# Expert stage of an attention, mixture-of-experts and feed-forward kernel: another place for the decoding operations, for GpSimd's weight blocks and for the decoded part's subtraction

## Chip, core and metric

The kernel runs on one core of one Trainium2 chip. The metric is the device time of one execution in microseconds (us), as the median of several runs. Five engines work side by side, each through its own instructions in order: TensorE (PE; its weight loads are listed as PEld), VectorE (DVE), ScalarE (ACT), GpSimd (POOL) and SyncE (SP), which here only issues DMAs.

## What is computed

Three layers follow each other. A gated linear attention over 4 x 8 heads of 768 positions gives 3072 tokens of 384 values. A mixture of experts sends each token that is not skipped to one of 8 experts. A feed-forward layer with a maximum over three products ends the kernel. The change is in the second layer, where some weights of the third are decoded on the side.

```python
for e in range(E):                      # 8 experts, w1[e] 384 x 1024, w2[e] 1024 x 384
    mask = e_idx == e
    h = np.maximum(xc[mask] @ w1[e], 0.0)
    y[mask] = gate_w[mask, None] * (h @ w2[e])
out[do_compute] = xc + y
...
h = np.maximum(np.maximum(x @ w1, x @ w2), x @ w3)   # 384 x 768 each
return h @ w_out                                     # 768 x 384
```

## The kernel before

Every float32 product is made of three products of float32r values: a tensor is split into a high part, which ScalarE writes as a cast copy, and a low part, source minus high part, written by VectorE or GpSimd. `split` (L119) does both; its two operations carry the lines L120 and L121.

**Expert stage.** The loop at L765 makes 66 steps; step s serves expert e = s // 8 and block f = s % 8 of 128 hidden units, and has up to 256 token slots as columns. In a step TensorE runs `gemm1(s)`, nine matmuls (L661 to L663) into one of three PSUM banks named `ph`, and `gemm2(s - 2)`, six matmuls into two banks `po` (L679 to L681). After `gemm1`, ScalarE writes `hh`, the high part of the rectified result (L666), and VectorE writes `hl`, the low part (L667). In steps f = 4, 5 and 6 `xprep` (L638) also transposes one third of the next expert's tokens and splits it into `xh` and `xl`; the one of f = 5 takes a `ph` bank. So the bank of `gemm1` of block 4 comes back at `gemm1` of block 6, once `hl` of block 4 is written. At f = 1 the expert before is finished: two VectorE operations write its rows `o` from PSUM (L688), and GpSimd scatters them with two indirect DMAs (L689). After the last expert `merge` (L728) forms its tokens' rows directly for the third layer.

**Weights.** In step s `wsplit` (L440) splits the weight block of step s + 3 into `wh` and `wl`, 128 x 768 each. A set of f says whether VectorE or GpSimd subtracts; ScalarE always casts. Four blocks share one buffer `raw` of 1.5 MB, of which there are two; at f = 0 and f = 4, behind the split of a buffer's last block, `wload` (L431) loads it anew for the blocks five steps ahead.

**Decoding.** `mdecs` (L601) is a generator that decodes the third layer's weights in 12 units of 128 x 768, in pieces that end at a `yield`. A unit takes: an absolute value on ScalarE (L101, in `begin`, which also issues the load `rm` of the next unit), two one-input operations on VectorE (`decode_exp`, L105 and L106, called exponent operations below), two operations with two inputs (`decode_bits`, L111 and L112, called bit operations), a cast copy to `mh` on ScalarE (L621), and the subtraction that gives `ml` (L624), on GpSimd for the first seven units (`EARLY`). Stores of `mh` and `ml` (L628) follow for some units. `decode_to(n)` (L760) runs the generator up to piece n; the loop calls it at the head of a step, with a count that grows by one every two steps from step 3 on, so that a unit takes eight steps.

The order on each engine is the order in which the Python code issues instructions.

Of the kernel before, what the change touches and what calls it, by code (L numbers as in the profile page):

```python
# [9 lines left out]
F32 = mybir.dt.float32  # L10
F32R = mybir.dt.float32r
BF16 = mybir.dt.bfloat16
I32 = mybir.dt.int32
U32 = mybir.dt.uint32
AF = mybir.ActivationFunctionType
ALU = mybir.AluOpType
# [25 lines left out]
NTILE = N // 128  # L42
EW = 768
AHEAD = 3
DEC = 3
UN = 768
ORDER = [(w, u) for u in range(2) for w in range(3)] + [(3, 0), (3, 1), (0, 2), (1, 2), (2, 2), (3, 2)]
EARLY = 7
# [31 lines left out]
K_LO = 2.0 ** -15  # L80
K_HI = 122880.0
# [3 lines left out]
def tile_gla_moe_moe2(ctx, tc, akq, vp, rp, wgt, cst, io, ew, md, out):  # L85
    nc = tc.nc
    V, A, G, T, SY = nc.vector, nc.scalar, nc.gpsimd, nc.tensor, nc.sync
# [8 lines left out]
    def words(raw):  # L96
        wd = raw.rearrange("p (n t) -> p n t", t=2)
        return wd[:, :, 0], wd[:, :, 1]

    def decode_abs(t, raw):  # L100
        A.activation(t, words(raw)[1], AF.Abs)  # L101

    def decode_exp(t):
        ti = t.bitcast(I32)
        V.tensor_scalar(t, t, K_LO, K_HI, ALU.max, ALU.min)  # L105
        V.tensor_scalar(ti, ti, 0x07FFFFFF, 3, ALU.bitwise_and, ALU.logical_shift_left)  # L106

    def decode_bits(t, raw):
        lo, hi = words(raw)
        ti = t.bitcast(I32)  # L110
        V.scalar_tensor_tensor(ti, hi.bitcast(I32), -0x40000000, ti, ALU.bitwise_and, ALU.bitwise_or)  # L111
        V.scalar_tensor_tensor(ti, lo.bitcast(I32), 29, ti, ALU.logical_shift_right, ALU.bitwise_or)  # L112

    def decode(t, raw):
        decode_abs(t, raw)
# [3 lines left out]
    def split(h, l, src, eng=None):  # L119
        A.copy(h, src)  # L120
        (eng or V).tensor_tensor(l, src, h.bitcast(F32), ALU.subtract)  # L121

    with tc.manual_schedule():
# [307 lines left out]
        def wload(n):  # L431
            rw[n] = rawp.tile([128, 4 * EW], F32, name="raw")
            SY.dma_start(out=rw[n], in_=ew[n // 2, :, n % 2 * 4 * EW:(n % 2 + 1) * 4 * EW])
# [6 lines left out]
        def wsplit(s, eng=None):  # L440
            h, l = (wsl.tile([128, EW], F32R, name=f"w{a}") for a in "hl")
            split(h, l, rw[s // 4][:, s % 4 * EW:(s % 4 + 1) * EW], eng)
            wr[s] = h, l
# [144 lines left out]
        rm = {}  # L588
# [7 lines left out]
        def mload(i):  # L596
            rm[i] = rmp.tile([128, 2 * UN], F32, name="rm")
            w, u = ORDER[i]
            SY.dma_start(out=rm[i].bitcast(I32), in_=md[3 * w + u].bitcast(I32))

        def mdecs():  # L601

            ts = {}

            def begin(i):
                if i < len(ORDER):
                    if i + 1 < len(ORDER):
                        mload(i + 1)
                    ts[i] = rmp.tile([128, UN], F32, name="dt")
                    decode_abs(ts[i], rm[i])  # L610

            begin(0)
            yield
            for i, (w, u) in enumerate(ORDER):
                z = slice(u * UN, (u + 1) * UN)
                t, h, l = ts[i], mh[w][:, z], ml[w][:, z]
                decode_exp(t)
                yield
                decode_bits(t, rm[i])
                yield  # L620
                A.copy(h, t)  # L621
                begin(i + 1)
                yield
                (G if i < EARLY else V).tensor_tensor(l, t, h.bitcast(F32), ALU.subtract)  # L624
                for k in range(k3 if w < 3 else 0):
                    if (w, k) in ONE:
                        for j, m in enumerate((mh, ml)):
                            SY.dma_start(out=wv[ONE[w, k]][:, 2 * u:2 * u + 2, j],  # L628
                                         in_=mv(m[w], k)[:, 2 * u:2 * u + 2].bitcast(F32))
                    if u == 2:  # L630
                        A.copy(fv(blk[w, k])[:, 4:], t.rearrange("p (f k c) -> k p f c", f=2, k=k3)[k])
                yield

        def xload(e):
            xs_[e] = xp.tile([128, 2, XW], F32, name="xs", bufs=3)
            SY.dma_start(out=xs_[e], in_=slots[e * CAP:(e + 1) * CAP, :].rearrange("(m p) d -> p m d", p=128))

        def xprep(e, k):  # L638
            xs = xs_[e]
            if k < 0:  # L640
                ix_[e] = xp.tile([128, 2, 1], I32, name="ix", bufs=4)
                V.tensor_copy(ix_[e], xs[:, :, DM + 1:DM + 2])
                return
            if k == 0:
                xh_[e] = xhp.tile([128, k3, CAP], F32R, name="xh")
                xl_[e] = xhp.tile([128, k3, CAP], F32R, name="xl")
            pt = (bank(ps_h, "ph") if k == 1 else bank(ps_t, "pt"))[:, 0:CAP]
            for m in range(2):
                T.transpose(pt[:, m * 128:(m + 1) * 128], xs[:, m, k * 128:(k + 1) * 128], ident)
            split(xh_[e][:, k, :], xl_[e][:, k, :], pt)  # L650
# [61 lines left out]
        def gstart(k):  # L712
            pm.append(bank(ps_o, f"po{k}") if k < 2 else bank(ps_t, "pt"))
            for c in range(4):
                T.matmul(pm[k][:, c * 128:(c + 1) * 128], xg_[0][:, c, k * 128:(k + 1) * 128], ident,
                         start=(c == 0), stop=False)
# [43 lines left out]
        def decode_to(n):  # L760
            while ndec[0] < n:
                ndec[0] += 1
                next(dec, None)

        for s in range(ns + LAG):  # L765
            e, f = divmod(s, nf1)
            if s >= DEC:
                decode_to(min(s - DEC + 1, 58) * (4 * EARLY + 1) // 58 + max(s - 60, 0))
            if s < ns:
                if 4 <= s + AHEAD < ns:  # L770
                    wsplit(s + AHEAD, V if f in (0, 2, 4, 5, 7) or s < 2 else G)
                if s and (s + AHEAD) % 4 == 3 and (s + AHEAD) // 4 + 2 < 2 * NE:
                    wload((s + AHEAD) // 4 + 2)
                if f == XL and e + 2 < NE:
                    xload(e + 2)
                if s == 0:
                    xload(1)
                    xload(0)
                gemm1(s)
            if s in (ns - 1, ns):  # L780
                gstart(s - ns + 1)
            if s == ns + 1:
                gstart(2)
            if s >= LAG:
                gemm2(s - LAG)
            x0 = XP if e else 5
            if e + 1 < NE and x0 <= f < x0 + k3:
                xprep(e + 1, f - x0)
            if f == IX and e < NE:
                xprep(e, -1)  # L790
            if s == ns - 7:
                gload(0)
            if s == ns - 3:
                sel = select()
            if s == 9:
# [114 lines left out]
        lo, hi = {}, {}  # L910
# [55 lines left out]
        def alljobs():  # L966
            yield from wjobs()
            yield GAP
            xslots()
            yield from xjobs(0)  # L970
# [3 lines left out]
        def pump(us):  # L974
            debt[0] += us
            while debt[0] > 0:
                c = next(jobs, None)
                debt[0] = 0.0 if c is None else debt[0] - c
# [110 lines left out]
        for g in range(ng):  # L1089
            for f in range(nf2):  # L1090
                if g == 1 and f == 0:
                    rawt += [rawp.tile([128, 8 * DM], F32R, name="raw") for _ in range(2)]
                gemm1(g, f)
                if g == 0:
                    decode_to(4 * EARLY + 10 + 4 * f)
                    if f == 3:
                        decode_to(99)
                        rmt += [rmp.tile([128, 2 * UN], F32, name="rm") for _ in range(2)]
                        for _ in jobs:
                            pass  # L1100
                        jobs, debt[0] = alljobs(), 0.0
                if g == 0 and f == 0:
                    xgload(0, 1)
                    xgload(1, 3)
                if g == 0 and f == nf2 - 1:
                    xgload(0, 2, A)
                if pend is not None:
                    gemm2(*pend)
                    pump(PUMP[3] if g or f > 3 else 0)
                pend = (g, f)  # L1110
                if g == 0 and 2 <= f < 2 + k3:
                    pt = bank(ps_t, "pt")
                    tr(0, f - 2, pt)
                    split(xh_[1][:, f - 2, :], xl_[1][:, f - 2, :], pt)
                if g == 1 and f == LOADAT:
                    wdload(0)
# [250 lines left out]
```

## Time and profile before

| quantity | value |
|---|---|
| median of 3 runs | 587.48 us (587.32 to 589.78) |
| profiled execution, own time | 588.17 us |
| its span, first to last instruction | 586.3 us |
| TensorE busy | 563.4 us (96%) |
| VectorE busy | 440.5 us (75%) |
| ScalarE busy | 296.7 us (51%) |
| GpSimd busy | 247.6 us (42%) |
| mean granted TensorE clock | 0.996 of full speed |

The profile is one execution. Every row has a start and a duration in us from the span's start, and idle time is put down to the instruction that ended it. TensorE's ends are modelled, so its busy time can hide a short stop; the distance between the first matmuls of two steps does not. The expert stage runs from about 142 to 297 us.

### The profile page before, as it was taken

How to read it: one execution, taken by the hardware profiler on the slowest of the kernel's cores; microseconds unless marked ns; L12 is line 12 of the kernel's file. 1: busy time of each engine (PE TensorE's matmuls, PEld its weight loads, DVE VectorE, ACT ScalarE, POOL GpSimd, SP SyncE). 2: the span in 40 equal slices, each digit the busy share in tenths (PEclk: the TensorE clock that was granted, in tenths of full speed). 3: DMA queues.
4: the chain of work that ended last, by engine and by line, in shares of the span. 5: the costliest groups of instructions: out<-in, count | busy, mean ns of one | idle time of the engine just before them, and what ended most of it. 6: DMA issues, size and time to landing. Idle time of an engine off the chain costs nothing.

```text
span 586.3 us, 10712 instructions
## 1 busy us (share of the span) xinstructions
PE 563.4 (96%) x3995; PEld 504.0 (86%) x3995; DVE 440.5 (75%) x747; ACT 296.7 (51%) x602; POOL 247.6 (42%) x202
## 2 busy tenths in 40 slices
PE   6999999999999989998999999999999999999995
PEld 3888888888899989998978788888878899888895
DVE  7899999977788898889768898593767684766700
ACT  2655575654566556665324435454453474454310
POOL 6554598752465346544321213122464401455410
PEclk8999999999999999999999999999999999999999
DMA  8889998935687879784508239515663623565011
GB/s 314 308 237 351 306 309 320 331 116 190 239 256 288 300 259 312 263 308 169 180 20 267 74 108 354 212 39 207 210 242 137 217 108 137 187 213 192 0 56 59
DMA packets 50973, 123.04 MB, mean 210 GB/s; under 512 B 4546, under 2 KB 38832, under 8 KB 47328
## 3 DMA queue, kind: packets, MB, share of 16 engines
q1 hardware_dynamic: 47824, 116.65, 57.8%
q0 software_dynamic: 2560, 4.83, 2.2%
q10 hardware_dynamic: 528, 0.79, 0.5%
q8 instruction: 33, 0.54, 0.4%
q14 instruction: 28, 0.23, 0.1%
HBM read 93.03 MB, written 32.28 MB: 214 GB/s over the span
## 4 chain that ended last, share of the span: by engine, by line
PE 58%; DVE 11%; issue 4%; ACT 3%; DMA 3%; POOL 1%; DVEq 0%; ACTq 0%; POOLq 0%
PE po L1004 3%; PE po L1005 3%; PE po L1006 3%; PE ph L1004 3%; PE ph L1005 3%; PE ph L1006 3%; PE ph L661 3%; PE po L681 2%; PE ph L662 2%; PE po L679 2%; PE po L680 2%; PE ph L663 2%; DVE wl L121 2%; PE ph L843 2%; PE ph L842 2%
## 5 line engine op out<-in xcount | busy, mean ns | idle before, releaser
L121 POOL TENSOR_TENSOR wl<-raw,wh 128x768 fp32r<-128x768 f32 x26 | 49.2, 1893 | 64.0 <-ACT wh L120 63.9
L121 DVE TENSOR_TENSOR wl<-raw,wh 128x768 fp32r<-128x768 f32 x38 | 57.5, 1513 | 11.7 <-ACT wh L120 11.7
L120 ACT CAST wh<-raw 128x768 fp32r<-128x768 f32 x64 | 53.4, 834 | 21.7 <-DMA raw<-in_ew_dram 11.1
L661 PE MATMUL ph<-xh,wh 128*128 128x256 f32 x192 | 56.5, 294 | 3.6 <-DVE hl L667 3.5
L662 PE MATMUL ph<-xl,wh 128*128 128x256 f32 x192 | 54.4, 283 | 0.4 <-DVE xl L121 0.3
L663 PE MATMUL ph<-xh,wl 128*128 128x256 f32 x192 | 54.3, 283 | 0.0
L679 PE MATMUL po<-wh,hh 128*128 128x384 f32 x128 | 43.5, 340 | 0.0
L681 PE MATMUL po<-wh,hl 128*128 128x384 f32 x128 | 43.2, 338 | 0.0
L680 PE MATMUL po<-wl,hh 128*128 128x384 f32 x128 | 43.1, 337 | 0.0
L661 PEld LDWEIGHTS ph<-xh,wh 128*128 128x128 f32 x192 | 36.5, 190 | 5.4 <-DVE hl L667 5.2
L268 PE MATMUL ps<-q,k 64*128 64x128 f32 x384 | 32.9, 292 | 8.1 <-POOL q L243 4.1
L228 POOL TENSOR_TENSOR k<-akq,sf 128x512 f32<-128x512 f32 x24 | 28.5, 1187 | 24.6 <-DVE sf L225 16.1
L268 PEld LDWEIGHTS ps<-q,k 64*128 64x128 f32 x384 | 27.0, 193 | 12.4 <-POOL q L243 5.2
L662 PEld LDWEIGHTS ph<-xl,wh 128*128 128x128 f32 x192 | 36.4, 190 | 0.8 <-DVE xl L121 0.8
L663 PEld LDWEIGHTS ph<-xh,wl 128*128 128x128 f32 x192 | 36.4, 189 | 0.0
L419 POOL DMA_INDIRECT slots<-xr,si x24 | 24.4, 1015 | 27.2 <-DVE xr L416 11.9
L667 DVE SCALAR_TENSOR_TENSOR hl<-ph,hh 128x256 fp32r<-128x256 f32 x64 | 26.5, 417 | 9.2 <-ACT hh L666 8.9
L666 ACT ACTIVATE hh<-ph 128x256 fp32r<-128x256 f32 x64 | 24.5, 383 | 14.9 <-PE ph L663 13.6
L225 DVE TENSOR_TENSOR_SCAN sf<-akq,pcs 128x520 f32<-128x520 f32 x24 | 29.4, 1224 | 3.0 <-DMA akq<-in_akq_dram 2.7
L239 DVE TENSOR_TENSOR_SCAN ap<-akq,pcs 128x521 f32<-128x521 f32 x24 | 29.8, 1241 | 2.2
L274 DVE TENSOR_TENSOR sm<-ps,cs 128x512 f32<-128x512 f32 x48 | 30.3, 672 | 0.0
L243 POOL TENSOR_TENSOR q<-akq,ap 128x512 f32<-128x512 f32 x24 | 28.4, 1183 | 4.5 <-DVE ap L239 2.8
(659 smaller groups left out, 1721.9 us busy)
## 6 DMA issues: line engine op xcount, KB each, us to landing
raw<-in_ew_dram SPq DMA_DIRECT2D x15, 1536.0 KB, 6.6
akq<-in_akq_dram SPq DMA_DIRECT2D x22, 772.5 KB, 6.6
rm<-in_md_dram SPq DMA_DIRECT2D x12, 768.0 KB, 7.8
mh<-wd SPq DMA_DIRECT2D x7, 1024.0 KB, 4.9
ml<-wd SPq DMA_DIRECT2D x7, 896.0 KB, 6.8
raw<-wd SPq DMA_DIRECT2D x6, 1024.0 KB, 5.0
raw<-wd SPq DMA_DIRECT2D x6, 896.0 KB, 6.5
vt<-in_vp_dram SPq DMA_DIRECT2D x24, 200.0 KB, 6.8
```

The lines of the kernel that those rows point to most:

```text
L120: A.copy(h, src)
L121: (eng or V).tensor_tensor(l, src, h.bitcast(F32), ALU.subtract)
L268: T.matmul(ps[i][:, p, :], kh[j][r0:r0 + 64, p, :], qh[j][r0:r0 + 64, p, :], start=True, stop=True)
L661: T.matmul(ph, wh[:, z], xh_[e][:, k, :], start=(k == 0), stop=False)
L662: T.matmul(ph, wh[:, z], xl_[e][:, k, :], start=False, stop=False)
L663: T.matmul(ph, wl[:, z], xh_[e][:, k, :], start=False, stop=(k == k3 - 1))
L679: T.matmul(po, hh[:, zm], wh, start=(f == 0), stop=False)
L680: T.matmul(po, hh[:, zm], wl, start=False, stop=False)
L681: T.matmul(po, hl[:, zm], wh, start=False, stop=(f == nf1 - 1))
L1004: T.matmul(bk, uh, vh, start=start, stop=False, skip_group_check=not start)
L1005: T.matmul(bk, uh, vl, stop=False, **more)
L1006: T.matmul(bk, ul, vh, stop=True, **more)
```

## The change

The generator's pieces for the first seven units are made smaller and are placed by block: one VectorE operation at a time. `decode_to` moves from the head of a step to its end, behind `gemm2` and `xprep`, starts at step 8 and runs one piece a step, so that a unit fills the eight steps of one expert: exponent operations at f = 1 and f = 2, bit operations at f = 3 and f = 5, `begin` at f = 6, and at f = 0 of the next expert the copy, GpSimd's subtraction and the stores. GpSimd's weight blocks are split at f = 1, 4 and 6, where they were at f = 1, 3 and 6.

```diff
-DEC = 3
+DEC = 8
...
-    def decode_exp(t):
+    def decode_exp(t, parts=(0, 1)):
         ti = t.bitcast(I32)
-        V.tensor_scalar(t, t, K_LO, K_HI, ALU.max, ALU.min)
-        V.tensor_scalar(ti, ti, 0x07FFFFFF, 3, ALU.bitwise_and, ALU.logical_shift_left)
+        if 0 in parts:
+            V.tensor_scalar(t, t, K_LO, K_HI, ALU.max, ALU.min)
+        if 1 in parts:
+            V.tensor_scalar(ti, ti, 0x07FFFFFF, 3, ALU.bitwise_and, ALU.logical_shift_left)
...
-                decode_exp(t)
-                yield
-                decode_bits(t, rm[i])
-                yield
-                A.copy(h, t)
-                begin(i + 1)
-                yield
-                (G if i < EARLY else V).tensor_tensor(l, t, h.bitcast(F32), ALU.subtract)
+                if i < EARLY:
+                    decode_exp(t, (0,))
+                    yield
+                    decode_exp(t, (1,))
+                    yield
+                    decode_bits(t, rm[i], (0,))
+                    yield
+                    yield
+                    decode_bits(t, rm[i], (1,))
+                    yield
+                    begin(i + 1)
+                    yield
+                    yield
+                    A.copy(h, t)
+                    G.tensor_tensor(l, t, h.bitcast(F32), ALU.subtract)
+                else:
...
         for s in range(ns + LAG):
             e, f = divmod(s, nf1)
-            if s >= DEC:
-                decode_to(min(s - DEC + 1, 58) * (4 * EARLY + 1) // 58 + max(s - 60, 0))
             if s < ns:
                 if 4 <= s + AHEAD < ns:
-                    wsplit(s + AHEAD, V if f in (0, 2, 4, 5, 7) or s < 2 else G)
+                    wsplit(s + AHEAD, V if f in (0, 2, 3, 5, 7) or s < 2 else G)
...
                 xprep(e, -1)
+            if s >= DEC:
+                decode_to(min(s - DEC + 1, 8 * EARLY + 1) + max(s - 60, 0))
...
-                    decode_to(4 * EARLY + 10 + 4 * f)
+                    decode_to(8 * EARLY + 10 + 4 * f)
```

How the instructions stand on two engines, before and now (line numbers of the changed kernel are higher: its L125 is L121, L635 is L624, L687 is L667, L106 and L108 are L105 and L106, L114 is L111, L708 and L709 are L688 and L689).

GpSimd before, through most of an expert, from the block at f = 1 to that of f = 6:

```order
L121 TENSOR_TENSOR wl_2741<-raw_2592,wh_2740 128x768
L689 DMA x2_63<-o_2764,ix_2683 3072x384
L689 DMA x2_63<-o_2769,ix_2683 3072x384
L121 TENSOR_TENSOR wl_2806<-raw_2592,wh_2805 128x768
L624 TENSOR_TENSOR ml1_2220<-dt_2531,mh1_2216 128x768
L121 TENSOR_TENSOR wl_2901<-raw_2715,wh_2900 128x768
```

GpSimd now, from the end of f = 0 to the block at f = 6:

```order
L635 TENSOR_TENSOR ml0_2219<-dt_2477,mh0_2215 128x768
L125 TENSOR_TENSOR wl_2737<-raw_2581,wh_2736 128x768
L709 DMA x2_63<-o_2760,ix_2671 3072x384
L709 DMA x2_63<-o_2765,ix_2671 3072x384
L125 TENSOR_TENSOR wl_2824<-raw_2581,wh_2823 128x768
L125 TENSOR_TENSOR wl_2887<-raw_2705,wh_2886 128x768
```

The subtraction of the decoded part stood behind the block of f = 3, and stands now ahead of the block of f = 1 and of the two indirect DMAs.

VectorE before, from f = 0 to f = 5 (`o` are the finished expert's rows):

```order
L121 TENSOR_TENSOR wl_3203<-raw_2963,wh_3202 128x768
L667 SCALAR_TENSOR_TENSOR hl_3219<-ph_3208,hh_3218 128x256
L667 SCALAR_TENSOR_TENSOR hl_3243<-ph_3232,hh_3242 128x256
L688 SCALAR_TENSOR_TENSOR o_3252<-po0_3042,xs_2656 128x384
L688 SCALAR_TENSOR_TENSOR o_3257<-po1_3043,xs_2656 128x384
L121 TENSOR_TENSOR wl_3268<-raw_3083,wh_3267 128x768
L667 SCALAR_TENSOR_TENSOR hl_3282<-ph_3271,hh_3281 128x256
L667 SCALAR_TENSOR_TENSOR hl_3308<-ph_3297,hh_3307 128x256
L121 TENSOR_TENSOR wl_3323<-raw_3083,wh_3322 128x768
L667 SCALAR_TENSOR_TENSOR hl_3339<-ph_3328,hh_3338 128x256
L121 TENSOR_TENSOR xl_3349<-pt_3350,xh_3348 128x256
L121 TENSOR_TENSOR wl_3356<-raw_3206,wh_3355 128x768
```

VectorE now, from the finished expert's rows at f = 1 to the block of f = 5:

```order
L708 SCALAR_TENSOR_TENSOR o_3248<-po0_3034,xs_2644 128x384
L708 SCALAR_TENSOR_TENSOR o_3253<-po1_3035,xs_2644 128x384
L106 TENSOR_SCALAR dt_3166<-dt_3166 128x768
L125 TENSOR_TENSOR wl_3260<-raw_3072,wh_3259 128x768
L687 SCALAR_TENSOR_TENSOR hl_3274<-ph_3263,hh_3273 128x256
L108 TENSOR_SCALAR dt_3166<-dt_3166 128x768
L125 TENSOR_TENSOR wl_3287<-raw_3072,wh_3286 128x768
L687 SCALAR_TENSOR_TENSOR hl_3301<-ph_3290,hh_3300 128x256
L114 SCALAR_TENSOR_TENSOR dt_3166<-rm_2919,dt_3166 128x768
L687 SCALAR_TENSOR_TENSOR hl_3328<-ph_3317,hh_3327 128x256
L125 TENSOR_TENSOR xl_3338<-pt_3339,xh_3337 128x256
L125 TENSOR_TENSOR wl_3345<-raw_3196,wh_3344 128x768
```

The weight block ahead of `hl` of block 4 is gone from there; three decoding operations, which stood elsewhere in the expert, now stand between the rows `o` and that `hl`, with one weight block at f = 2 and one at f = 3.

ScalarE before, at the stage's end, up to the merge (`mh` is the copy, `dt` the absolute value, `hh` of steps 61 to 63):

```order
L666 ACTIVATE hh_4061<-ph_4051 128x256
L666 ACTIVATE hh_4083<-ph_4073 128x256
L666 ACTIVATE hh_4112<-ph_4102 128x256
L621 CAST mh3_2218<-dt_3994 128x768
L101 ACTIVATE dt_4127<-rm_3992 128x768
L666 ACTIVATE hh_4139<-ph_4129 128x256
L732 ACTIVATE wh_4095<-po0_4014,xs_3635 128x384
```

ScalarE now, in the same place:

```order
L686 ACTIVATE hh_4074<-ph_4064 128x256
L101 ACTIVATE dt_4087<-rm_3893 128x768
L686 ACTIVATE hh_4106<-ph_4096 128x256
L634 CAST mh3_2218<-dt_3895 128x768
L686 ACTIVATE hh_4130<-ph_4120 128x256
L641 CAST mh3_2218<-dt_4087 128x768
L101 ACTIVATE dt_4163<-rm_4085 128x768
L752 ACTIVATE wh_4091<-po0_4006,xs_3621 128x384
```

The copy and the absolute value of the last two units stood ahead of the last `hh`, and stand now behind it, next to the merge.

## Rows read from the trace of the kernel before

**Rows 1.** Stretches by expert: length, PE, PEld, DVE, ACT, POOL busy, clock, DMA, GB/s:

```profile
159.42:178.07 18.65, 18.34 (x130) 17.70 (x129) 16.72 (x32) 11.94 (x22) 9.59 (x6) 1.00 0.83 280
...
196.14:216.02 19.88, 18.23 (x128) 17.64 (x127) 17.45 (x26) 11.33 (x21) 9.37 (x6) 1.00 0.83 292
216.02:233.70 17.68, 17.68 (x127) 17.58 (x127) 15.17 (x22) 11.79 (x21) 10.04 (x6) 1.00 0.81 280
...
251.91:271.79 19.88, 18.23 (x128) 17.64 (x127) 17.02 (x25) 11.33 (x21) 9.34 (x6) 1.00 0.84 296
```

**Rows 2.** Timeline of TensorE, steps' first matmuls: start, duration, engine; bracketed, idle before:

```profile
210.88 0.39 PE L661 MATMUL ph<-xh,wh 128*128 128x256 f32 x1 [1.35 <-DVE hl L667]
...
224.55 0.29 PE L661 MATMUL ph<-xh,wh 128*128 128x256 f32 x1
...
229.16 0.36 PE L661 MATMUL ph<-xh,wh 128*128 128x256 f32 x1
```

**Rows 3.** Timeline of VectorE, then of GpSimd, expert 3, from block 3 on:

```profile
206.19 4.30 DVE L121 TENSOR_TENSOR wl<-raw,wh 128x768 fp32r<-128x768 f32 x1 [0.30 <-ACT wh L120]
210.42 0.41 DVE L667 SCALAR_TENSOR_TENSOR hl<-ph,hh 128x256 fp32r<-128x256 f32 x1
...
206.00 1.87 POOL L121 TENSOR_TENSOR wl<-raw,wh 128x768 fp32r<-128x768 f32 x1
207.81 1.85 POOL L624 TENSOR_TENSOR ml<-dt,mh 128x768 fp32r<-128x768 f32 x1
```

**Rows 4.** Timeline of SyncE, experts 2 and 3, and of ScalarE, expert 3:

```profile
193.03 0.43 SPq L433 DMA_DIRECT2D raw<-in_ew_dram  x1
...
200.37 0.34 SPq L433 DMA_DIRECT2D raw<-in_ew_dram  x1
200.76 0.42 SPq L599 DMA_DIRECT2D rm<-in_md_dram  x1
...
200.76 0.83 ACT L120 CAST wh<-raw 128x768 fp32r<-128x768 f32 x1 [2.96 <-DMA raw<-in_ew_dram]
```

**Rows 5.** Instructions by tile: ns min/median/max, first and last start, form:

```profile
L105 DVE TENSOR_SCALAR dt<-dt x8: 542/549/1812, 155.8 to 284.5; 128x768 f32<-128x768 f32 x8
...
L111 DVE SCALAR_TENSOR_TENSOR dt<-rm,dt x8: 944/948/951, 160.7 to 286.6; 128x768 int32<-128x768 int32 x8
...
L101 ACT ACTIVATE dt<-rm x8: 887/926/937, 164.9 to 289.4; 128x768 f32<-128x768 f32 x8
...
L121 DVE TENSOR_TENSOR wl<-raw,wh x34: 941/953/4304, 159.2 to 281.4; 128x768 fp32r<-128x768 f32 x34
```

**Rows 6.** Timeline of GpSimd and VectorE, third layer's first step:

```profile
305.85 1.81 POOL L121 TENSOR_TENSOR hb0l<-hf,hb0h 128x512 fp32r<-128x512 f32 x1 [3.98 <-ACT hb0h L120]
...
306.54 1.93 DVE L112 SCALAR_TENSOR_TENSOR dt<-rm,dt 128x768 int32<-128x768 int32 x1
```

**Rows 7.** Timelines of ScalarE, VectorE and GpSimd, expert 7, from 271.79:

```profile
273.05 0.39 ACT L666 ACTIVATE hh<-ph 128x256 fp32r<-128x256 f32 x1 [0.22 <-PE ph L663]
274.15 0.84 ACT L120 CAST wh<-raw 128x768 fp32r<-128x768 f32 x1 [0.71 <-PE po L681]
...
276.14 1.13 DVE L688 SCALAR_TENSOR_TENSOR o<-po,xs 128x384 f32<-128x384 f32 x2
...
278.74 0.97 POOL L689 DMA_INDIRECT x<-o,ix  x1 [0.30 <-issue]
```

**Rows 8.** From issue to landing, all loads of `raw`, then of `rm`:

```profile
DMA to landing us min/median/max: 6.3/6.6/10.4
...
DMA to landing us min/median/max: 4.2/7.8/9.6
```

**Rows 9.** SyncE's load for the third layer, its first use, ScalarE's merge:

```profile
281.25 0.36 SPq L699 DMA_DIRECT2D raw<-x  x1
...
287.95 0.89 PE po L715 x8
...
293.31 1.10 ACT L732 ACTIVATE wh<-po,xs 128x384 fp32r<-128x384 f32 x2 [2.79 <-PE po L681]
```

More of the change, by code (lines that the diff above doesn't have):

```diff
@@ L101, in decode_abs, with decode_bits @@
         A.activation(t, words(raw)[1], AF.Abs)
-    def decode_exp(t):
+    def decode_exp(t, parts=(0, 1)):
         ti = t.bitcast(I32)
-        V.tensor_scalar(t, t, K_LO, K_HI, ALU.max, ALU.min)
-        V.tensor_scalar(ti, ti, 0x07FFFFFF, 3, ALU.bitwise_and, ALU.logical_shift_left)
-    def decode_bits(t, raw):
+        if 0 in parts:
+            V.tensor_scalar(t, t, K_LO, K_HI, ALU.max, ALU.min)
+        if 1 in parts:
+            V.tensor_scalar(ti, ti, 0x07FFFFFF, 3, ALU.bitwise_and, ALU.logical_shift_left)
+    def decode_bits(t, raw, parts=(0, 1)):
         lo, hi = words(raw)
         ti = t.bitcast(I32)
-        V.scalar_tensor_tensor(ti, hi.bitcast(I32), -0x40000000, ti, ALU.bitwise_and, ALU.bitwise_or)
-        V.scalar_tensor_tensor(ti, lo.bitcast(I32), 29, ti, ALU.logical_shift_right, ALU.bitwise_or)
+        if 0 in parts:
+            V.scalar_tensor_tensor(ti, hi.bitcast(I32), -0x40000000, ti, ALU.bitwise_and, ALU.bitwise_or)
+        if 1 in parts:
+            V.scalar_tensor_tensor(ti, lo.bitcast(I32), 29, ti, ALU.logical_shift_right, ALU.bitwise_or)
     def decode(t, raw):
@@ L616, in mdecs @@
                 t, h, l = ts[i], mh[w][:, z], ml[w][:, z]
-                decode_exp(t)
-                yield
-                decode_bits(t, rm[i])
-                yield
-                A.copy(h, t)
-                begin(i + 1)
-                yield
-                (G if i < EARLY else V).tensor_tensor(l, t, h.bitcast(F32), ALU.subtract)
+                if i < EARLY:
[14 more added lines that the diff above has]
+                else:
+                    decode_exp(t)
+                    yield
+                    decode_bits(t, rm[i])
+                    yield
+                    A.copy(h, t)
+                    begin(i + 1)
+                    yield
+                    V.tensor_tensor(l, t, h.bitcast(F32), ALU.subtract)
                 for k in range(k3 if w < 3 else 0):
```

## The prediction

> **What bounds the kernel now.** I read the stretches by expert first, then the start of each step on TensorE, then what stood ahead of the late ones on VectorE, GpSimd, ScalarE and SyncE.
>
> Six experts (1 to 6) run from 159.42 to 271.79, which is 112.37 us. The shortest takes 17.68, with TensorE busy throughout; experts 3 and 6 take 19.88 each, 2.20 more [rows 1]. The time is lost at one place. With t as the time from an expert's first matmul, block 4 of the unhindered expert starts at t = 224.55 - 216.02 = 8.53, four steps of 2.13, and block 6 at t = 229.16 - 216.02 = 13.14 [rows 2]. In expert 3 block 6 starts at 210.88, t = 14.74, 1.60 late, released by `hl` [rows 2]: it needs the `ph` bank of block 4, whose `hl` ran only at 210.42 [rows 3].
>
> That `hl` stood behind a weight block on VectorE that took 4.30 us, where an undisturbed one takes 0.95 [rows 3, 5]. Beside it GpSimd ran two subtractions without a gap, its weight block from 206.00 and the decoded part from 207.81 to 209.66; VectorE ended 0.83 later, which is one such operation [rows 3]. So a VectorE operation with two inputs in SBUF that meets GpSimd's subtraction waits until GpSimd has done all that is queued. The one-input decoding operations show it too: 549 ns in the median and 1812 at most [rows 5].
>
> Why experts 3 and 6 are worst: expert 2's decoded part has six stores, and they stand on SyncE behind GpSimd's subtraction and ahead of the next `raw` load, which so left at 193.03, t = 14.96 in expert 2. ScalarE then waited 2.96 us for it at 200.76 [rows 4]. That pushed GpSimd's block of f = 3 onto the VectorE block of f = 4.
>
> **The change, part by part.** No operation is added or dropped; five of eight blocks stay on VectorE. What counts is where each lands.
>
> *The stalls that can go.* 112.37 - 6 x 17.68 = 6.29 us [rows 1]. This is the ceiling of the gain: 17.68 is already TensorE without a gap.
>
> *The new places on GpSimd.* A step's cast starts 0.23 after the step's first matmul (274.15 against 271.79 + 2.13) and takes 0.84; `hh` is done at 273.05 + 0.39, 1.65 after it [rows 7]. So in the new order the copy of the decoded part runs on ScalarE at t = 1.65 to 2.48, with the 0.83 of a cast of its size [rows 4]; GpSimd subtracts it from 2.5 to 4.4 and the block of f = 1, whose cast is ready at 3.3, from 4.4 to 6.3, at 1.85 each [rows 3]. The pair without a gap is still there; it has moved from f = 3 and 4 to f = 0 and 1. The two scatters follow, at 6.4 and 7.7, and end at 8.7 [rows 7].
>
> *The new places on VectorE.* The finished expert's rows start at t = 276.14 - 271.79 = 4.35 and take 1.13 [rows 7]. The first exponent operation arrives at 5.48 and waits for GpSimd until 6.3: this is now the operation that is held, 0.8 us, and what is queued behind it is the block of f = 2, `hl` of block 2, the second exponent operation, the block of f = 3, `hl` of block 3, a bit operation and then `hl` of block 4. With 0.55, 0.95, 0.41, 0.55, 0.95 and 0.41 [rows 3, 5], each starting 0.07 before the one ahead ends (206.19 + 4.30 against 210.42 [rows 3]), the bit operation arrives at 9.7. GpSimd's block of f = 4 has its cast at 8.53 + 0.23 + 0.84 = 9.6 and takes its turn as VectorE's block ends, at about 9.65. If GpSimd is first, it runs to 11.5, the bit operation ends at 12.45, and `hl` of block 4 ends at 12.8; it is needed at 13.14. If VectorE is first, all is earlier. **So the sum has a margin of 0.35 us per expert here, and I expect no stall.** Later in the expert VectorE has one block (f = 5), one bit operation, three `xl` and one block (f = 7) in 7 us, and nothing falls due.
>
> *The `raw` load of f = 4* now waits for GpSimd's block, until 11.5 where it left at 14.96. Landing takes 6.6 in the median [rows 8], so it is there at 18.1; ScalarE wants it at 17.68 + 2.13 + 0.23 = 20.04. The wait of 2.96 goes.
>
> *An exponent operation beside a scatter* is in no row of before. The second one arrives at 8.0 while a scatter runs until 8.7 [rows 7]. If they do not disturb each other: nothing. If it waits 0.7 us: the block of f = 3 ends at 10.1, GpSimd's subtraction at 11.95, the bit operation at 12.85 and `hl` at 13.2, late by about 0.13, for six experts 0.8 us. If the first exponent operation also holds the first scatter for 0.5: 1.2 us in all, `hl` late by 0.6, for six experts 3.6. I take 0.8, the middle case, since one-input operations do wait for GpSimd in other places [rows 5]. The Trainium skill ("SBUF — State Buffer", "SBUF: two separate sides") states that GpSimd cannot write the descriptors of its own DMAs while VectorE runs an operation in a two-port mode. By that rule, which no run here has shown yet, the sum would be the one with 3.6 at worst and not the one with nothing.
>
> *The merge.* In steps 61 to 65 the pieces crowd. With expert 7 at 271.79, step 62's copy on ScalarE ends at t = 15.3 and GpSimd's last subtraction at 17.15; the four operations of the next unit (0.55, 0.55, 0.95, 0.95 [rows 5]) end at 20.0, its copy at 20.8, the next absolute value (0.93 [rows 5]) at 21.7. The merge's first operation stood at t = 21.52, waiting for TensorE [rows 9]; it is now queued behind that absolute value: 0.2 us late. If `rm`, issued at about 13.4, lands after 9.6 [rows 8], it is 2.4 late. I take 0.2, since little else is loaded there.
>
> *The third layer's first load* leaves when the last scatter has landed, 281.25, 1.54 after that scatter's end at 279.71 [rows 7, 9]. The scatter now ends at t = 8.7 and not 7.92, so the load leaves 0.8 later; with 4.2 of landing [rows 8] it had 2.5 to spare before 287.95 [rows 9] and keeps 1.7. Nothing.
>
> **Sum:** -6.3 + 0.8 + 0.2 = -5.3 us. The third layer behind it is the same work and moves as a whole. The profiled execution, 588.17, would become 582.9; the median is 0.69 below that execution, so 587.48 becomes **582.2**. About 0.5% (2.9 us) is what a measurement of this kernel can tell from no change: faster is below 584.5.
>
> **Rivals.**
>
> *The bit operation becomes the held one.* The bit operations never met GpSimd in an expert (951 ns at most [rows 5]); where one met it in the third layer it took 1.93 [rows 6]. Now both stand where GpSimd's blocks of f = 4 and 6 run. Above, 0.7 us of wait made 0.13 of stall; a wait of 1.5 ahead of the bit operation makes 0.9, for six experts 5.6, and 587.5 is left: no change. Against it: that much waiting has no owner in the rows beyond the 1.2 counted.
>
> *Slower: the order of loads.* `rm` left right behind the `raw` load of f = 0 (200.37, 200.76 [rows 4]); now it waits for the second bit operation and leaves at about t = 17.1, 2.9 us ahead of that `raw` load, at 2.35 of the next expert. The cast of f = 5 wants the block at about t = 11.1. ScalarE's `hh` of block 5 is queued behind it, and `hl` of block 5, due at 15.5, has some 1.2 us to spare behind that; a block that is 4 us late costs about 1.6 per expert, for six 9.9, and gives 587.5 - 6.1 + 9.9 = 591.3. It decides from 12.5 us of landing on; the longest was 10.4 [rows 8]. For it: `rm` took up to 9.6. Against it: it took that behind a `raw` load, so both together were there within 10 us of the first issue, and a head start of 2.9 leaves `raw` about 7.
>
> *The merge is blocked by a late `rm`.* 2.2 us more than in the sum: 584.4.
>
> **How the numbers follow.** Forecast 0.68 (581 to 585, its unknown between 0 and 3.6 us with the point at 0.8); no change by the bit operation 0.20 (585 to 589); merge late 0.05; slower 0.07. Faster takes the first but for 0.01 and the third: 0.72; same takes that 0.01 and the second: 0.21; slower 0.07. The range starts at 580.9, where all 6.3 us come and the load before the stage helps a little, and reaches into the second case, to 586.5; about 2 in 10 lie outside.
>
> **What would show it.** Right: experts 1 to 6 at 17.7 to 17.9 us each; no VectorE block over 3 us; the held operation is the first exponent operation, about 1.3 us; no ScalarE wait for `raw` over 1 us; GpSimd's decoded subtraction directly ahead of the block of f = 1. Wrong: TensorE released by `hl` at block 6 in every expert, with a bit operation of 1.9 to 2.8 us ahead of it (first rival); `raw` waits at f = 5 (second); an idle TensorE ahead of the merge's matmuls (third). The forecast falls if the scatters hold VectorE for more than the 1.2 us counted.

## The result, and the profile after

The changed kernel takes 582.76 us (median of 6 runs, 581.70 to 583.78) where the kernel before takes 587.53 (6 runs, 587.24 to 589.78). The medians are 4.8 us apart; the ratio is 0.9909, with a 95% interval of 0.9892 to 0.9926, so after is 0.9% faster. Forecast were 582.2 us and a range of 580.9 to 586.5.

The profiled execution of after has a span of 579.9 us, 6.4 less than before. Cut at first matmuls, both profiles divide like this:

| stretch (us) | before | after | difference |
|---|---|---|---|
| to the first matmul of expert 0 | 142.42 | 141.10 | -1.32 |
| expert 0, to the first matmul of expert 1 | 17.00 | 17.31 | +0.31 |
| experts 1 to 6 | 112.37 | 106.74 | -5.63 |
| expert 7 and the merge, to the third layer's first matmul | 25.49 | 25.71 | +0.22 |
| the rest | 289.0 | 289.0 | 0.0 |

The first line is attention, which the change doesn't touch. Over the profiles of after and of the ten kernels below this stretch lies between 141.10 and 144.00, always with the same instructions in it.

Expert 0's +0.31 belongs to the change, by the move of GpSimd's block from f = 3 to f = 4. Expert 0 takes 17.26 to 17.41 us in the kernels with the blocks at f = 1, 4 and 6 (after, e2, e5, e6, e7, e10) and 16.99 to 17.05 in those with 1, 3 and 6 (before, e1, e3, e4, e8); e9 alters this expert itself. Where the block of f = 3 is VectorE's, its subtraction still runs when the last of attention's scatters, which reach into expert 0, starts, and that scatter takes 1.30 us where it took 0.97 (VectorE and GpSimd of after, then GpSimd of before):

```profile
146.89 0.96 DVE L125 TENSOR_TENSOR wl<-raw,wh 128x768 fp32r<-128x768 f32 x1 [0.39 <-ACT wh L124]
...
147.39 1.30 POOL L423 DMA_INDIRECT slots<-xr,si  x1 [0.30 <-issue]
...
148.72 0.97 POOL L419 DMA_INDIRECT slots<-xr,si  x1 [0.31 <-issue]
```

The first load `xs` of token rows leaves as this scatter has landed, 9.05 us after the stage's first matmul and not 8.73, and TensorE waits 1.19 us for it and not 0.86. So the change is worth the second, third and fourth lines, -5.1 us. The experiments are compared by the length of six experts, which the part ahead can't disturb.

Stretches by expert, after, that answer to [rows 1] (length, PE, PEld, DVE, ACT, POOL busy, clock, DMA, GB/s), with the six of them together:

```profile
158.41:176.62 18.21, 18.14 (x130) 17.68 (x129) 13.16 (x33) 11.90 (x22) 9.67 (x5) 1.00 0.68 246
...
158.41:265.15 106.74, 106.67 (x761) 105.53 (x760) 79.59 (x149) 70.95 (x127) 62.77 (x35) 1.00 0.84 291
```

Expert 2 takes 17.78, experts 3 to 6 take 17.70, 17.69, 17.67 and 17.69. TensorE is busy for 106.67 of 106.74 us. VectorE was busy for 15.2 to 17.5 us an expert [rows 1] and is for 13.2 to 13.3 now, with the same work: its operations hardly stand and wait for GpSimd any more.

Timeline of VectorE, then of GpSimd, expert 4 (first matmul at 212.10), that answers to [rows 3]:

```profile
216.34 1.13 DVE L708 SCALAR_TENSOR_TENSOR o<-po,xs 128x384 f32<-128x384 f32 x2
217.39 1.26 DVE L106 TENSOR_SCALAR dt<-dt 128x768 f32<-128x768 f32 x1
218.57 0.95 DVE L125 TENSOR_TENSOR wl<-raw,wh 128x768 fp32r<-128x768 f32 x1
...
219.77 0.54 DVE L108 TENSOR_SCALAR dt<-dt 128x768 int32<-128x768 int32 x1
220.24 0.94 DVE L125 TENSOR_TENSOR wl<-raw,wh 128x768 fp32r<-128x768 f32 x1
...
221.44 0.94 DVE L114 SCALAR_TENSOR_TENSOR dt<-rm,dt 128x768 int32<-128x768 int32 x1
222.33 0.42 DVE L687 SCALAR_TENSOR_TENSOR hl<-ph,hh 128x256 fp32r<-128x256 f32 x1
...
214.57 1.85 POOL L635 TENSOR_TENSOR ml<-dt,mh 128x768 fp32r<-128x768 f32 x1 [3.34 <-ACT mh L634]
216.37 1.85 POOL L125 TENSOR_TENSOR wl<-raw,wh 128x768 fp32r<-128x768 f32 x1
218.38 1.13 POOL L709 DMA_INDIRECT x<-o,ix  x1 [0.15 <-issue]
219.81 1.34 POOL L709 DMA_INDIRECT x<-o,ix  x1 [0.30 <-DVE wl L125]
221.81 2.28 POOL L125 TENSOR_TENSOR wl<-raw,wh 128x768 fp32r<-128x768 f32 x1 [0.65 <-ACT wh L124]
```

The `hl` of block 4 starts at 222.33, t = 10.23; it is needed at 13.14. One VectorE operation is held by GpSimd, the first exponent operation at 217.39 (1.26 us), and three of GpSimd's are held by VectorE: the two scatters (1.13 and 1.34, 0.97 undisturbed) and the block of f = 4 (2.28, 1.85 undisturbed).

Tile `wl`, after, that answers to [rows 5] (ns min/median/max, first and last start):

```profile
L125 DVE TENSOR_TENSOR wl<-raw,wh x38: 943/952/959, 144.0 to 273.3; 128x768 fp32r<-128x768 f32 x38
```

No weight block on VectorE takes over 0.96 us, where the longest took 4.30. ScalarE's waits for `raw`, 11.1 us in all before, are not in the list of waits any more.

### The profile page after: what moved, and what is told of

Same layout as the page of the kernel before. It is cut to its first block, busy times and chain, and to the rows that moved or that the text cites. A ratio compares the mean times of both kernels' runs of the same rounds, so it can differ in the third digit from the quotient of the medians.

```text
span 579.9 us, 10728 instructions
## 1 busy us (share of the span) xinstructions
PE 561.4 (97%) x3995; PEld 502.7 (87%) x3995; DVE 419.3 (72%) x747; ACT 298.7 (52%) x602; POOL 256.0 (44%) x202
## 4 chain that ended last, share of the span: by engine, by line
PE 64%; DVE 12%; issue 3%; ACT 2%; DMA 2%; POOL 2%; DVEq 0%; POOLq 0%; ACTq 0%
PE ph L681 4%; PE ph L682 4%; PE ph L683 4%; PE po L701 3%; PE po L699 3%; PE po L700 3%; PE po L1024 3%; PE po L1025 3%; PE po L1026 3%; PE ph L1024 3%; PE ph L1025 3%; PE ph L1026 3%; PE ph L863 2%; PE ph L862 2%; PE ph L861 2%
## 5 line engine op out<-in xcount | busy, mean ns | idle before, releaser
L125 POOL TENSOR_TENSOR wl<-raw,wh 128x768 fp32r<-128x768 f32 x26 | 53.4, 2053 | 32.7 <-ACT wh L124 32.6
L125 DVE TENSOR_TENSOR wl<-raw,wh 128x768 fp32r<-128x768 f32 x38 | 36.2, 953 | 9.3 <-ACT wh L124 9.3
L687 DVE SCALAR_TENSOR_TENSOR hl<-ph,hh 128x256 fp32r<-128x256 f32 x64 | 26.8, 419 | 16.7 <-ACT hh L686 16.5
```

## The experiments

| kernel | subtraction of the decoded part | decoding on VectorE | GpSimd's blocks | six experts | ratio to before, 95% |
|---|---|---|---|---|---|
| before | behind block 3 | in pairs | 1, 3, 6 | 112.37 | |
| after | head of block 1 | one by one | 1, 4, 6 | 106.74 | 0.9909 (0.9892 to 0.9926) |
| e1 | head of block 1 | one by one | 1, 3, 6 | 106.88 | 0.9893 (0.9871 to 0.9915) |
| e2 | as before | in pairs | 1, 4, 6 | 111.78 | 1.0008 (0.9993 to 1.0023) |
| e3 | behind block 3 | one by one | 1, 3, 6 | 114.15 | 1.0020 (0.9998 to 1.0042) |
| e4 | as before, stores later | in pairs | 1, 3, 6 | 111.83 | 0.9984 (0.9969 to 1.0000) |
| e8 | f = 0, ahead of block 1 | in pairs | 1, 3, 6 | 113.57 | 1.0049 (1.0029 to 1.0068) |
| e10 | behind the scatters | one by one | 1, 4, 6 | 106.75 | 0.9910 (0.9882 to 0.9937) |

e1, e3, e5 to e7, e9 and e10 are edits of the kernel after, the others of the kernel before. e5, e6 and e7 have one run each, so they are read from their profiles.

**Only the placing of the decoding (e1).** The blocks on GpSimd are put back to 1, 3 and 6.

```diff
-                    wsplit(s + AHEAD, V if f in (0, 2, 3, 5, 7) or s < 2 else G)
+                    wsplit(s + AHEAD, V if f in (0, 2, 4, 5, 7) or s < 2 else G)
```

> The changed kernel with GpSimd's weight blocks back at f = 1, 3 and 6; the decoding stays one operation at a time. Measure: the time from expert 1's first matmul to expert 7's, 112.37 us before, 106.74 in the changed kernel. Theory A (the stall needs GpSimd's pair without a gap, block of f = 3 and decoded subtraction, beside VectorE's weight block just ahead of hl of block 4; the subtraction is no longer there, so one block alone holds VectorE until t = 11 at most and hl is ready by 12.5, due at 13.1): 106.7 to 107.5. Theory B (small pieces at the ends of steps do it all): 106.7. Theory C (the place of GpSimd's blocks does it): back to about 112.

It keeps the whole gain. Its six experts together, then expert 4 (first matmul at 214.65) on VectorE and GpSimd:

```profile
160.82:267.70 106.88, 106.80 (x761) 105.58 (x760) 98.59 (x148) 71.30 (x127) 57.75 (x35) 1.00 0.84 290
```

```profile
223.12 3.30 DVE L114 SCALAR_TENSOR_TENSOR dt<-rm,dt 128x768 int32<-128x768 int32 x1
226.35 0.95 DVE L125 TENSOR_TENSOR wl<-raw,wh 128x768 fp32r<-128x768 f32 x1
227.22 0.41 DVE L687 SCALAR_TENSOR_TENSOR hl<-ph,hh 128x256 fp32r<-128x256 f32 x1
...
222.37 1.34 POOL L709 DMA_INDIRECT x<-o,ix  x1 [0.30 <-DVE wl L125]
223.73 1.87 POOL L125 TENSOR_TENSOR wl<-raw,wh 128x768 fp32r<-128x768 f32 x1
```

VectorE is busy for 98.59 us, 19 more than in after, and most of that is time in which the bit operations are held (medians of 2091 and 2147 ns, 948 and 950 in after): here one takes 3.30 us. But one block is queued behind it and not a pair, and `hl` of block 4 is done at 227.63, 0.16 ahead of block 6, which starts at 227.79 with no wait. So the move of the block buys slack on VectorE (3.2 us an expert), and no time; in expert 0 it costs 0.3 us (16.99 in e1, 17.31 in after).

**Only the move of the block (e2).**

```diff
-                    wsplit(s + AHEAD, V if f in (0, 2, 4, 5, 7) or s < 2 else G)
+                    wsplit(s + AHEAD, V if f in (0, 2, 3, 5, 7) or s < 2 else G)
```

> The kernel before with only GpSimd's blocks moved, to f = 1, 4 and 6; the decoding as before, two operations at a time at the heads of steps. Six experts, 112.37 before. Theory A: the pair is still without a gap (subtraction about t = 8.9 to 10.7, block of f = 4 to 12.6), but what it holds is VectorE's block of f = 5, behind hl of block 4, and block 6 starts on time: 106.7 to 108.0. Theory B: about 112. Theory C: 106.7.

The expectation missed: 111.78 us, and no difference in time. VectorE and GpSimd, expert 4, and TensorE's wait for `hl` (us in total, times, longest):

```profile
221.10 0.96 DVE L121 TENSOR_TENSOR wl<-raw,wh 128x768 fp32r<-128x768 f32 x1 [0.47 <-ACT wh L120]
...
222.48 5.09 DVE L121 TENSOR_TENSOR wl<-raw,wh 128x768 fp32r<-128x768 f32 x1
...
220.79 1.00 POOL L689 DMA_INDIRECT x<-o,ix  x1 [0.16 <-DVE o L688]
222.09 0.98 POOL L689 DMA_INDIRECT x<-o,ix  x1 [0.30 <-DVE wl L121]
223.08 1.86 POOL L624 TENSOR_TENSOR ml<-dt,mh 128x768 fp32r<-128x768 f32 x1
224.89 1.85 POOL L121 TENSOR_TENSOR wl<-raw,wh 128x768 fp32r<-128x768 f32 x1
```

```profile
PEld po L681 <- DVE hl L667: 6.1, 6, 1.9
```

The pair on GpSimd is still there, the subtraction now ahead of block 4, and VectorE's block of f = 3 meets it. That block starts 0.60 us ahead of the subtraction and should have gone first by that; it ends 0.83 after the pair instead, and takes 5.06 to 5.11 us at six of seven places (3.17 at the other).

**Small pieces, subtraction where it was (e3).** Decoding starts five steps earlier, which puts the subtraction behind GpSimd's block of f = 3 again; the blocks are the old ones.

```diff
-DEC = 8
+DEC = 3
...
-                    wsplit(s + AHEAD, V if f in (0, 2, 3, 5, 7) or s < 2 else G)
+                    wsplit(s + AHEAD, V if f in (0, 2, 4, 5, 7) or s < 2 else G)
```

> The changed kernel's small pieces at the ends of steps, with DEC = 3 and the old blocks, so that the decoded subtraction follows GpSimd's block of f = 3 directly, as before the change, and the stores stand ahead of the raw load of f = 4 again. Six experts. Theory A: the stall is back, VectorE's block of f = 4 takes 2.5 to 4.3 us and the six experts 109.5 to 112.5. Theory B: 106.7 to 107.3. Theory C: about 112.

The stall comes back: 114.15 us. The block of f = 4 on VectorE beside the pair on GpSimd in expert 6, and the wait:

```profile
261.56 4.85 DVE L125 TENSOR_TENSOR wl<-raw,wh 128x768 fp32r<-128x768 f32 x1 [1.03 <-ACT wh L124]
...
260.94 0.98 POOL L709 DMA_INDIRECT x<-o,ix  x1 [0.30 <-DMA raw<-in_ew_dram]
261.94 1.87 POOL L125 TENSOR_TENSOR wl<-raw,wh 128x768 fp32r<-128x768 f32 x1
263.74 1.85 POOL L635 TENSOR_TENSOR ml<-dt,mh 128x768 fp32r<-128x768 f32 x1
```

```profile
PEld ph L681 <- DVE hl L687: 5.6, 5, 2.3
```

That is the 4.30 us of [rows 3] once more. The stores stand ahead of the `raw` load again too, and ScalarE waits for `raw` for up to 3.2 us, so e3 alone does not part the pair from the late load. Against after it differs in the step at which the decoding stands, and in the old blocks, which cost nothing in e1. So the rival that small pieces alone do it falls.

**Loads on time, all else as before (e4).** A unit's stores are issued one piece later, so that they stand behind the `raw` load on SyncE and not ahead of it.

```diff
+            def stores():
+                while held:
+                    o, a = held.pop(0)
+                    SY.dma_start(out=o, in_=a)
...
                 decode_exp(t)
+                stores()
...
-                            SY.dma_start(out=wv[ONE[w, k]][:, 2 * u:2 * u + 2, j],
-                                         in_=mv(m[w], k)[:, 2 * u:2 * u + 2].bitcast(F32))
+                            held.append((wv[ONE[w, k]][:, 2 * u:2 * u + 2, j],
+                                         mv(m[w], k)[:, 2 * u:2 * u + 2].bitcast(F32)))
```

> The kernel before with the stores of a decoded part issued one piece later (f = 6), so that the raw load of f = 4 is not queued behind them and behind GpSimd's subtraction. The GpSimd pair stays. Theory A with the load as its amplifier: the loads leave about 2 us earlier, ScalarE's waits for raw fall under 1 us, experts 3 and 6 come down from 19.88 to 17.7 to 18.4 and the six to 108.0 to 109.5. Rival (the load's lateness does not matter, the pair alone makes 19.88): 112 and experts 3 and 6 unchanged.

The waits for `raw` fall from 11.1 us to 4.3 (the longest from 3.2 to 0.9), and yet the six experts take 111.83: the expected 108 to 109.5 is missed. VectorE and GpSimd in expert 4, and what TensorE waits for:

```profile
217.41 0.95 DVE L111 SCALAR_TENSOR_TENSOR dt<-rm,dt 128x768 int32<-128x768 int32 x1
218.40 0.96 DVE L112 SCALAR_TENSOR_TENSOR dt<-rm,dt 128x768 int32<-128x768 int32 x1
219.28 2.62 DVE L121 TENSOR_TENSOR wl<-raw,wh 128x768 fp32r<-128x768 f32 x1
...
226.33 3.81 DVE L121 TENSOR_TENSOR wl<-raw,wh 128x768 fp32r<-128x768 f32 x1 [1.07 <-ACT wh L120]
...
219.09 1.98 POOL L121 TENSOR_TENSOR wl<-raw,wh 128x768 fp32r<-128x768 f32 x1 [4.54 <-ACT wh L120]
...
225.65 1.87 POOL L121 TENSOR_TENSOR wl<-raw,wh 128x768 fp32r<-128x768 f32 x1
227.45 1.87 POOL L630 TENSOR_TENSOR ml<-dt,mh 128x768 fp32r<-128x768 f32 x1
```

```profile
PEld po L689 <- DVE hl L675: 2.7, 3, 1.0
PEld ph L669 <- DVE hl L675: 2.2, 3, 0.8
```

With the load on time the old collision is smaller, and another comes in. The two bit operations in a row push VectorE's block of f = 0 back to 219.28, and GpSimd's block of f = 1, at 219.09, is just ahead of it. Experts 2, 4 and 6 lose 2.6 us together by that, at block 3; the same experts still meet the old pair (3.81 us at 226.33), and their block 6 is late by 2.2 us together, 0.8 at most. In before block 6 was late by 4.3 us over the six experts, 1.8 at most (counted from the distance to the first matmul of the block ahead, 2.34 for block 6 and 2.13 for block 3 in the unhindered expert). So with the load on time about half of the old stall goes, and two bit operations in a row cost as much again.

**Only the subtraction's place (e8).** In the kernel before, the subtraction and the stores alone go to the head of the next expert.

```diff
-                (G if i < EARLY else V).tensor_tensor(l, t, h.bitcast(F32), ALU.subtract)
...
+                if i < EARLY:
+                    held.append((i, w, u, t, h, l))
+                else:
+                    low(i, w, u, t, h, l)
...
+                while held:
+                    low(*held.pop())
```

> The kernel before, blocks, piece sizes and heads of steps unchanged, with only the decoded subtraction and its stores moved from the head of f = 4 to the head of f = 0 of the next expert. Six experts, 112.37 before, 106.88 with all of the decoding's change (e1). Theory A2 (after e1 to e3: what counts is that GpSimd's second subtraction is no longer between the block of f = 3 and VectorE's block of f = 4): the block of f = 4 takes 2 us at most, the pair now holds VectorE's bit operations and block of f = 7 or 0, where nothing is due, and the six take 106.7 to 108. Theory B2 (the two-at-a-time pieces at the heads of steps also have to go, since the bit operations push the block of f = 0 into GpSimd's block of f = 1, as in e4): a stall of 0.5 to 1 us at f = 2 or 3 in most experts, 109.5 to 112.

Six experts take 113.57, and the kernel is 0.5% slower than before:

```profile
218.67 2.61 DVE L121 TENSOR_TENSOR wl<-raw,wh 128x768 fp32r<-128x768 f32 x1
...
218.09 2.37 POOL L121 TENSOR_TENSOR wl<-raw,wh 128x768 fp32r<-128x768 f32 x1 [2.41 <-ACT wh L120]
```

```profile
PEld po L691 <- DVE hl L677: 8.4, 6, 1.6
```

The pair at f = 3 and 4 is gone, and the collision of e4 is there in every expert from the second on, at f = 0 and 1. With e1, e3 and e8 the gain is placed: it takes the subtraction away from block 3 and, with it, the bit operations away from the head of an expert. Neither half alone gains anything.

**How much room is left (e5, e6).** The first exponent operation, which changes nothing when it is repeated, runs twice and four times.

```diff
                     decode_exp(t, (0,))
+                    decode_exp(t, (0,))
```

> The changed kernel with the first exponent operation issued twice in every unit (the clamp gives the same values again), so that VectorE's chain ahead of the bit operation at f = 3 is 0.55 us longer. Theory A by the worked-out places: the bit operation now arrives at t = 9.9, just behind GpSimd's block of f = 4 (9.65), is held and takes 2.2 to 2.8 us; hl of block 4 starts at 12.3 to 12.5, due at 13.1; six experts 106.7 to 107.5. Rival (the margin of 0.35 us in the prediction was too kind, the bit operation stalls TensorE as soon as it is held): 109 or more.

> The same with the first exponent operation four times, 1.65 us more VectorE work per expert, 1.65 of some 11 us in 17.7. Theory A: the block of f = 3 itself now comes behind the start of GpSimd's block of f = 4, is held to 11.5, and the bit operation and hl of block 4 follow at 13.0 to 14.0: a stall of 0.5 to 1.2 us in each of the six experts, 109.5 to 114 in all. Rival (only VectorE's mean load counts, and that is still under 75%): 106.7 to 107.5.

With one more (0.55 us) six experts take 106.75, with three more (1.65) 113.17. In expert 4 of e5 (first matmul at 215.07):

```profile
225.00 2.44 DVE L114 SCALAR_TENSOR_TENSOR dt<-rm,dt 128x768 int32<-128x768 int32 x1
227.36 0.41 DVE L688 SCALAR_TENSOR_TENSOR hl<-ph,hh 128x256 fp32r<-128x256 f32 x1
...
224.77 1.84 POOL L125 TENSOR_TENSOR wl<-raw,wh 128x768 fp32r<-128x768 f32 x1 [0.78 <-ACT wh L124]
```

GpSimd's block now is 0.23 ahead of the bit operation, which is held; `hl` of block 4 ends at t = 12.70, 0.44 ahead of block 6 at 228.21. This is the order in which the prediction said "GpSimd is first", with an end at 12.8. In e6, expert 4 (first matmul at 216.98), the block of f = 3 itself is the one that is late (VectorE, GpSimd, TensorE's wait):

```profile
226.97 2.60 DVE L125 TENSOR_TENSOR wl<-raw,wh 128x768 fp32r<-128x768 f32 x1
...
226.69 2.06 POOL L125 TENSOR_TENSOR wl<-raw,wh 128x768 fp32r<-128x768 f32 x1 [1.01 <-ACT wh L124]
...
229.95 0.44 PE L704 MATMUL po<-wh,hl 128*128 128x384 f32 x1 [0.51 <-DVE hl L690]
```

Experts 2 to 6 then take 18.72 to 18.74, 1.05 more, and expert 1 takes 19.50. Between 0.55 and 1.65 us of further VectorE work an expert the gain is gone.

**The subtraction behind the scatters (e10).** All decoding moves two steps on.

```diff
-DEC = 8
+DEC = 10
```

> The changed kernel with DEC = 10: the same pieces two steps later, so that GpSimd's decoded subtraction, with its inputs ready at t = 6.8, stands directly behind the second scatter (about 6.8 to 7.8), and VectorE's block of f = 3 starts during that scatter, at about 7.5. Queue theory (from e2, where such a block took 5.1 us in five of six experts: a subtraction that is ready behind a scatter already keeps VectorE out while the scatter runs): the block of f = 3 takes 2.8 to 4.9 us. Rival (whoever starts first has the way; a scatter does not count): 0.95 us, and the subtraction takes longer instead. Six experts by the queue theory 108 to 112, by the rival 106.7 to 107.5.

This was to test what e2 had shown, and it did so by half. VectorE, then GpSimd, expert 4:

```profile
220.13 2.82 DVE L125 TENSOR_TENSOR wl<-raw,wh 128x768 fp32r<-128x768 f32 x1 [0.78 <-ACT wh L124]
...
219.26 0.98 POOL L709 DMA_INDIRECT x<-o,ix  x1 [0.30 <-DVE wl L125]
220.25 1.88 POOL L635 TENSOR_TENSOR ml<-dt,mh 128x768 fp32r<-128x768 f32 x1
```

By the records the block of f = 3 starts before the subtraction and ends 0.82 after it, as expected. The expected stall of TensorE did not come, 106.75 us: GpSimd's next block, at 222.37, starts 0.24 us behind the subtraction's end, so there is one operation to wait for and not two.

**The ends of the stage (e7, e9).** e7 caps the pieces of the stage at 59, so that those that crowd its last steps come later; e9 starts expert 1's transposes one step later and does the last of them at the end of expert 0.

```diff
-                decode_to(min(s - DEC + 1, 8 * EARLY + 1) + max(s - 60, 0))
+                decode_to(min(min(s - DEC + 1, 8 * EARLY + 1) + max(s - 60, 0), 8 * EARLY + 3))
```

> The changed kernel with the decoding stopped at its 59th piece until the third layer, so that no copy and no absolute value stand on ScalarE ahead of the merge; three pieces more fall into the third layer's first step. Prediction's term of 0.2 us: TensorE's gap of 0.34 us ahead of the merge's matmuls shrinks to 0.1 or less, the merge comes 0.2 us earlier after expert 7. If the third layer's first steps have no room on VectorE for the pieces, more than 0.2 us is lost there and the whole is slower by up to 2 us; if they have, the whole is 0.2 us faster, which the time alone cannot tell.

```diff
-            x0 = XP if e else 5
+            x0 = XP if e else 6
...
+                if not e and f == nf1 - 1:
+                    xprep(e + 1, 2)
```

> The changed kernel with expert 1's three transposes at f = 6, 7 and 7 of expert 0, where they were at 5, 6 and 7: TensorE waits 1.2 to 1.3 us there for the token rows to land (first expert, not touched by the change). From TensorE's first expert matmul to expert 1's: 17.31 us in the changed kernel. If the wait is only for the load: 16.0 to 16.4, less up to 0.6 that comes back as a wait for xl at expert 1's first block. If the load lands no earlier against the steps (it is the step at f = 6 that then waits): 17.0 to 17.3. The whole: 0.5 to 1.3 us faster than the changed kernel, about 0.2%.

In e7 expert 7 and the merge take 25.52 us, 0.2 less than in after, but what was put off comes back in the third layer's first step, where ScalarE's second copy of `hf` stands at 41.73 us from expert 7's first matmul and not at 39.40, and all behind the merge takes 2.8 us more; its one run took 584.58. In e9 expert 0 takes 15.97 us where after takes 17.31; 582.00 us (4 runs; 0.9884, 0.9860 to 0.9907) is the lowest median of all, and its interval overlaps that of after: not shown to be better by time.

## Why the prediction was right, and where not

**The ceiling, -6.29.** Measured -5.63. The difference is not the disturbance that I had added. Of the 0.66 that remains over six times 17.68, 0.53 is in expert 1. Its first step takes 0.44 longer than the others' and waits for `xl`; in before this step was 0.67 longer, with the same wait, and the change doesn't aim at it. The ceiling took every deviation from 17.68 for the same stall, and it was 0.7 too large, 0.5 of it by expert 1.

**The layout.** All places came within 0.4 us. From the first matmul of expert 4: GpSimd's subtraction at 2.47 (2.5 forecast), its block of f = 1 at 4.27 (4.4), the scatters at 6.28 and 7.71 (6.4 and 7.7), the end of the second at 9.05 (8.7), the rows at 4.24 (4.35), the bit operation at 9.34 (9.7), the block of f = 4 on GpSimd at 9.71 (9.65). The held operation is the first exponent operation, 1.26 us (about 1.3). The dead heat at f = 4 went VectorE's way, and in e5 the other way, where `hl` ended at 12.70 (12.8).

**An exponent operation beside a scatter, +0.8.** This term was 0 for TensorE. The second exponent operation took 0.54 us, undisturbed; the scatters took 1.13 and 1.34, where 0.97 was the price [rows 7]. So the scatter is the one that waits. The Trainium skill ("SBUF — State Buffer", "SBUF: two separate sides") says that GpSimd cannot write its DMA descriptors while VectorE runs in a two-port mode. On who waits the trace agrees with it (1.34 us against 0.97), though no run shows in which mode the operation ran. What the sum made of a held scatter was wrong: 3.6 at worst, by a scatter that ends later and pushes back all of GpSimd. It ended 0.35 later than laid out, and GpSimd then still stood idle for 0.65, waiting for the cast of block 4.

**The merge, +0.2.** Measured +0.22. ScalarE, after, that answers to [rows 9], with TensorE's first merge matmul:

```profile
286.09 0.91 ACT L101 ACTIVATE dt<-rm 128x768 f32<-128x768 f32 x1
286.91 1.02 ACT L752 ACTIVATE wh<-po,xs 128x384 fp32r<-128x384 f32 x2
...
287.52 0.49 PE L758 MATMUL po<-wh 128*128 128x512 f32 x1 [0.34 <-ACT wh L752]
```

The operation stood 2.79 us waiting for TensorE [rows 9] and now runs right behind the absolute value, and TensorE waits 0.34 for it. e7 takes the two operations away and gains 0.2.

**Expert 0, no term.** The sum has nothing for expert 0, and the change costs 0.31 there: the block of f = 3, now on VectorE, holds a scatter of attention. The prediction asked what VectorE does to the scatters within an expert, and not at the stage's start.

**The loads.** The third layer's first load leaves 10.54 us after the first matmul of expert 7, where it left at 9.46: 1.08 later and not 0.8, and nothing waits for it. The rival by which `rm` holds up the `raw` load of f = 5 did not come: from issue to landing `rm` took 8.3 us at most and `raw` 10.1, short of the 12.5 from which it decides. That a late `raw` load made experts 3 and 6 the worst is borne out by e4: with most of the lateness gone block 6 is late by 0.8 us at most and not 1.8. That this time would then be gained is not, since the bit operations collide instead.

**The rival of the bit operation.** It is held in e1 (3.30 us) and in e5 (2.44), without loss in either. In e1 the block of f = 3 no longer stands ahead of it on VectorE, and in e5 the 0.44 that is left is the margin of 0.35 that the prediction had for this order. On the prediction's scale (0.7 us of wait makes 0.13 of stall) the 1.65 of e6 makes 1.08, and e6 shows 1.05. The size agrees, but by another order: in e6 GpSimd holds VectorE's block of f = 3, where the prediction's case has that block hold GpSimd and the bit operation wait.

**The sum.** -5.63 + 0.31 + 0.22 = -5.1 against -5.3 forecast. The mechanism was right. That the sum is within 0.2 is partly luck: a ceiling 0.7 too high, a term of 0.8 that wasn't there and 0.3 in expert 0 that was not thought of nearly cancel. The median fell by 4.8; the part ahead of the stage alone varies by up to 2.9 us between profiles.

## What to carry to other kernels

Before work is moved between two engines, lay out one period of both from its first matmul, with each start and its due time, and look for two-input VectorE operations that meet two GpSimd operations in a row. A collision that is taken away at one place gives nothing until the queue behind it has a place free of the next one: here either half of the change alone was no gain. Where all stalls are gone, measure the room left by doubling a harmless operation; here it was between 0.55 and 1.65 us of 17.7. And look at the ends of a stage too: the move of one block, which gained nothing in the middle, cost 0.3 us at the start.

## What was not expected of the hardware

A two-input VectorE operation that starts while a scatter runs is let through or not by what stands behind the scatter. In e2 the block at 221.10 takes 0.96 us beside the first scatter, which another scatter follows. In after the block at 220.24 takes 0.94 beside the second scatter, behind which GpSimd stands idle for 0.65. The block at 222.48 of e2, beside the second scatter, waits for the subtraction that follows at 223.08, though it started 0.60 us earlier, and for the one behind that. Its end is 0.83 us after GpSimd's last; in e1, e3 and e10 this distance is 0.82 in the same situation, with starts 0.61, 0.38 and 0.12 us ahead of the GpSimd operation that follows the scatter (223.12, 261.56, 220.13). Whether VectorE is already kept out while the scatter runs, or loses the turn when it ends, the records don't tell; that the earlier recorded start does not decide it is shown by four kernels.

The other way round a one-input exponent operation of 0.54 us that was running as a scatter started lengthened it from 0.97 to 1.34 us and was not lengthened itself. The two-input block in expert 0 did the same, 0.96 us itself and 1.30 for the scatter.
